# Attention, experts and dense layers in one kernel: position products by their reader, W1 pieces by the sum's copy, stacked products for the last head, tiles moved by 32 bytes

## The chip, the cores and the metric

The kernel runs on one core of a Trainium2 chip. The core has TensorE (products and transposes, in the profile PE, its weight loads PEld), VectorE (DVE), ScalarE (ACT), GpSimd (POOL) and SyncE (SP), which here issues DMAs; DMAs are also issued from ScalarE's and GpSimd's queues. The metric is the time of one execution on the device in microseconds; of several executions the median counts.

## The reference

Three stages follow one another: attention in which a query sees only keys of its own cluster, a top-1 mixture of experts with a capacity, and a gated dense layer. All data are float32.

```python
# attention: batch 2, heads 8, sequence 768, head size 64, 16 clusters
mask = q_assign[:, :, :, None] == k_assign[:, :, None, :]       # nearest centroid of each
scores = np.where(mask, scale * np.matmul(q, k.transpose(0, 1, 3, 2)), -1e9)
attn = np.exp(scores - scores.max(-1, keepdims=True))
attn = attn / (attn.sum(-1, keepdims=True) + 1e-09)
x = np.matmul(attn, v)             # -> 1536 tokens of 512
# experts: 8 experts, hidden size 1024, capacity 384
logits = x @ w_gate
expert_idx = np.argmax(logits, axis=1)
gate_w = softmax(logits)[np.arange(N), expert_idx]
# token i takes the next free place of its expert; beyond the capacity it is dropped
h = np.maximum(np.einsum('ecd,edf->ecf', disp, w1), 0.0)
y = np.einsum('ecf,efd->ecd', h, w2)
out[i] = gate_w[i] * y[expert_idx[i], pos[i]]
# dense: hidden size 1536
g, val = x @ w_gate2, x @ w_val
return (g * sigmoid(g) * val) @ w_out
```

## The kernel before

**Attention.** Sixteen heads go in eight pairs. The work runs in 96 blocks g of 128 queries of one head (six blocks for a head, in two halves of three). The order within a block is written out as a list of tokens (`S`, `E`, `Q`, `T0`, `T1`, `B0`, `O`, `V0`, `B1`), which `run` (L448) walks: `Q` issues the score products of a later block (`qk`, L332: TensorE, then the row maximum `nm` on VectorE, L352), `S` its exps (`soft`, L355, ScalarE, L362), `T0` and `T1` transpose the exps P of this block, three 128x128 pieces each, into one of two PSUM buffers called `t` (`pt`, L365; L378); ScalarE copies the first out (L381), VectorE the second (L383). `V0` multiplies three blocks' transposes with the values (`pv`, L385): keys 0 to 383 add up on partitions 0 to 63 of `acc`, keys 384 to 767 on partitions 64 to 127. `E` adds the two (`evac`, L400): ScalarE copies the lower half to `ol` (L408), VectorE adds the upper (L410) into O, which holds two heads. `O` multiplies O with R, an identity beside the router's weights (`onat`, L414): out come the tokens' rows and their share of the router's logits.

**Routing.** Tokens are routed in four parts u = 0 to 3 of 384, each when the eight heads of its half sequence are done. `route` (L639) is a generator: `run` takes one step of it in each block (trickle, L503), so a chain is spread over some 16 blocks. It sums the logits over heads, finds the maximum, the one-hot rows `oh`, the gate `gw`, and the places: small products count the tokens of the same expert ahead of each token (L669 to L672). They are written into a `t` buffer when `oh` is done; VectorE reads that at L677, four steps on. Then x is scaled by the gate on ScalarE (L686) and GpSimd scatters the rows to memory (L624), and `offsets` (L697) turns the counts into places in memory. The parts 0 and 1 are routed in the middle of attention, 2 near its end, and 3 behind it: at the end of `run` the last two heads' second half is summed and multiplied (six copies with a scale on ScalarE instead of one product on VectorE, L435), with transposes of the identity as warming products in the gaps (`warm`, L442).

**Experts.** Weights come from memory in raw pieces of 512 KB in four buffers (`load`, L836), and are split in a high and a low part: ScalarE casts to W1h or W2h, VectorE or GpSimd subtracts (`split`, L846; half pieces for the first expert's W1 by `piece`, L857, one in each of the blocks 85 to 92). A product of two such numbers is three products, added in PSUM. `rows` (L868) loads an expert's tokens (`xr`), `xt` (L884) transposes them, twelve 128x128 pieces, into two banks and splits them into X; an `If` on the expert's count chooses the width 208 or 384 here, and 176, 208 or 384 in the layers (`arms`, L906). The 384-wide arm issues three products (`prod`, L916), the narrow arms two with the high and the low operand side by side (`both`, L925: 416 and 208 columns, or 352 and 176). `run` (L988) orders the experts: W1 in four steps (`l1`), W2 (`l2`). On SyncE's queue stand the raw loads, the first expert's rows (L876, two DMAs), two more raw loads, and the loads of counts into registers (L1007).

**Dense layers.** `gv` (L1130) multiplies the experts' outputs Yh and Yl with two weights (L1145), `o` (L1156) the hidden ghh and ghl with the last (L1165), all 512 columns wide.

**Places.** In the built program right-side tiles before the change start at multiples of 64 bytes within a partition: exps P 155584, their transposes PT 177088, the score operands Ak 118720 and Aq 106432, X 174784, H 187072, ghh 162496. The left side holds the weights, W1h 37984, W1l 54368, W2h 70752, W2l 87136, and Yh 103520, Yl 132192, each 32 past a multiple of 64.

Of the kernel before, what the change touches and what calls it, by code (L numbers as in the profile page):

```python
# [23 lines left out]
class Attention:  # L24


    def __init__(self, tc, ctx, q, k, v, cent, gate, keep, ident, raw):
# [30 lines left out]
        self.R = self.v1.tile([128, H // 2, 2 * D + 2 * E], F32, name="R")  # L58
        self.cbd = one.tile([128, H // 2, 2 * C], F32, name="cbd")
# [49 lines left out]
    def unit(self, gate):  # L109

        nc, ident = self.nc, self.ident
        H, D, E = self.H, self.D, self.E
        nc.gpsimd.memset(self.R[:, :, 2 * D:], 0.0)
        for r in range(2):
            o, c = slice(r * D, (r + 1) * D), slice(2 * D + r * E, 2 * D + (r + 1) * E)
            nc.sync.dma_start(out=self.R[o, :, c], in_=gate.rearrange("(h r d) e -> d r h e", d=D, r=2)[:, r])
        nc.gpsimd.tensor_copy(self.R[:, :, 0:2 * D], ident.unsqueeze(1).to_broadcast([128, H // 2, 2 * D]))

# [281 lines left out]
    def evac(self, G):  # L400
# [5 lines left out]
        acc = self.heads[hd]["acc"]  # L406
        ol = self.v1.tile([D, HS], F32, tag="ol", name="ol")
# [6 lines left out]
    def onat(self, n, half, act=None):  # L414
# [14 lines left out]
        x = self.x[2 * b + half][:, :, 2 * hp * D:2 * (hp + 1) * D].rearrange("p j (r d) -> p j r d", r=2)  # L429
        for dst, c, w in ((self.lg[:, b, js, 2 * hp:2 * hp + 2, :], 2 * D, E),  # L430
                          (x, 0, D)):
            if act and w == D:
                for jj in range(HJ):
                    for r in range(2):
                        act.activation(out=x[:, jj, r], in_=ps[:, jj, r * D:(r + 1) * D], func=AF.Copy,  # L435
                                       scale=rs[:, jj, r:r + 1])
                yield True
                return
            yield nc.vector.tensor_tensor(out=dst, in0=ps[:, :, c:c + 2 * w].rearrange("p j (r d) -> p j r d", r=2),
                                          in1=rs.unsqueeze(3).to_broadcast([128, HJ, 2, w]), op=ALU.mult)  # L440

# [6 lines left out]
    def run(self, cent, gate, early, fill, after, spare):  # L448
# [90 lines left out]
        assert not bg  # L539
        G, n = 2 * NH - 1, self.NP - 1  # L540
        (_, r), = chains
        assert not moves
        while next(r) is not True:
            pass
        self.pv(G)
        on = self.onat(n, 1, nc.scalar)
        for q, k in ((on, 2), (r, 9)):
            for _ in range(k):
                next(q)
        self.warm(self.ps_s, "s", 10)  # L550
# [3 lines left out]
        next(on)  # L554
        last = after(n, 1, lambda: self.warm(self.ps_s, "s", 16))
        next(last)
        for q in (on, last):
            for _ in q:
                pass
# [5 lines left out]
class Router:  # L565
# [73 lines left out]
    def route(self, u, sb, ps, idle=None):  # L639
# [16 lines left out]
        yield v.tensor_reduce(out=lo, in_=self.lg[:, b, js].rearrange("p j h e -> p j e h"), axis=AX.X, op=ALU.add)  # L656
        yield v.tensor_reduce(out=mx, in_=lo, axis=AX.X, op=ALU.max)
        yield v.tensor_tensor(out=d, in0=lo, in1=bc(mx), op=ALU.subtract)
        for j in range(J):
# [4 lines left out]
        yield v.tensor_tensor(out=oh, in0=t, in1=bc(m2), op=ALU.is_equal)  # L664
        if idle:
            idle()
        pt = ps.tile([128, J, 128], F32, tag="t", name="t")
        pp = pt.rearrange("p j t -> p (j t)")[:, 0:J * E].rearrange("p (j e) -> p j e", j=J)
        nc.tensor.matmul(flat(pp), lhsT=self.before, rhs=flat(oh), start=True, stop=False)  # L669
        for k in range(1, J):  # L670
            nc.tensor.matmul(flat(pp[:, k:]), lhsT=self.all, rhs=flat(oh[:, 0:J - k]), start=False, stop=False)
# [4 lines left out]
        yield True  # L676
# [108 lines left out]
class Experts:  # L785
# [50 lines left out]
    def load(self, i):  # L836
# [6 lines left out]
        self.nc.sync.dma_start(out=t, in_=src)  # L843
        self.loads[e, i] = t

    def split(self, e, i, low=None):  # L846
# [6 lines left out]
        j = (low or (nc.vector if i < 4 else nc.gpsimd)).tensor_tensor(out=l, in0=t, in1=h.bitcast(F32), op=ALU.subtract)  # L853
        self.load(8 * e + i + NRAW)
# [13 lines left out]
    def rows(self, e):  # L868
# [6 lines left out]
        for q, a, b in ((nc.sync, 0, 1), (nc.sync, 1, 3)) if e == 0 else ((nc.scalar, 0, 3),):  # L875
# [8 lines left out]
    def xt(self, e, cnt):  # L884
        nc = self.nc
        banks = []
        for kp in range(self.KD // 2):
            ps = self.bank("xp")
            for kk in range(2):
                c = (kp * 2 + kk) * 128  # L890
                for t in range(self.nt):
                    nc.tensor.transpose(ps[:, kk, t * 128:(t + 1) * 128], self.xr[e][:, t, c:c + 128], self.ident)
            banks.append(ps)

        def body(w):
            for kp, ps in enumerate(banks):
                h, l = [self.X[:, i, 2 * kp:2 * kp + 2, 0:w] for i in range(2)]
                nc.scalar.copy(out=h, in_=ps[:, :, 0:w])  # L898
                nc.vector.tensor_tensor(out=l, in0=ps[:, :, 0:w], in1=h.bitcast(F32), op=ALU.subtract)
# [66 lines left out]
    def l1(self, mp, cnt, last):  # L966
# [3 lines left out]
        def body(w):  # L970
            if last is not None:
# [310 lines left out]
```

## Time and profile before

| | before |
|---|---|
| median of three runs | 781.29 us (779.28 to 782.27) |
| profiled execution | 779.61 us |
| its span in the trace | 777.9 us |
| TensorE products | 751.8 us, 97% |
| weight loads | 624.7 us, 80% |
| VectorE | 513.7 us, 66% |
| ScalarE | 400.9 us, 52% |
| GpSimd | 272.1 us, 35% |
| granted clock over the span | 0.993 |

The span lies between the first and the last instruction; what is left of an execution, 1.7 us here, lies around it. Attention takes roughly the first 272 us, the experts the time up to about 500, the dense layers the rest. A busy share is an average over these stages: which wait matters is read from the waits and from the chain that ended last.

### The profile page before, as it was taken

The numbers are of one execution on the slowest core, as the hardware profiler recorded it, in microseconds if no ns is written. First come the engines' busy times: TensorE is split into PE (matmuls) and PEld (weight loads), VectorE is DVE, ScalarE is ACT, GpSimd is POOL, SyncE is SP. The second block draws the span as 40 slices with busy tenths as digits, with TensorE's granted clock in tenths as the row PEclk, the third lists the DMA queues.
The fourth block names the chain that finished last, engine by engine and source line by source line (L and its number), as shares of the span: only waits on it lengthen the run. The fifth ranks groups of instructions, "written<-read, shape, count | busy, mean of one in ns | idle before, by whom it ended". The sixth has DMA issues, their size and how long they took to land.

```text
span 777.9 us, 12611 instructions
## 1 busy us (share of the span) xinstructions
PE 751.8 (97%) x4298; PEld 624.7 (80%) x4298; DVE 513.7 (66%) x856; ACT 400.9 (52%) x772; POOL 272.1 (35%) x251
## 2 busy tenths in 40 slices
PE   8999999998999989999999999999999999999996
PEld 8777777776776679989999998788888888888885
DVE  4667778786786745667676655776667766767433
ACT  5777776776776844667666633444222232222110
POOL 6120220211221565444493432444223333233244
PEclk9999999999999999999999999999999999999999
DMA  8837768527153443777777632232122121110012
GB/s 202 211 81 202 197 191 236 133 72 183 41 153 119 149 151 108 254 241 248 259 248 250 215 110 82 82 108 82 55 65 71 56 80 55 55 54 1 1 54 109
DMA packets 93339, 102.35 MB, mean 132 GB/s; under 512 B 30304, under 2 KB 77408, under 8 KB 93248
## 3 DMA queue, kind: packets, MB, share of 16 engines
q1 hardware_dynamic: 88384, 89.33, 39.8%
q0 software_dynamic: 1920, 6.29, 2.2%
q10 hardware_dynamic: 2944, 5.54, 2.1%
q8 instruction: 55, 0.90, 0.5%
q14 instruction: 36, 0.29, 0.1%
HBM read 68.21 MB, written 12.58 MB: 104 GB/s over the span
## 4 chain that ended last, share of the span: by engine, by line
PE 77%; DVE 7%; ACT 7%; DMA 3%; issue 3%; POOL 1%; ACTq 0%; DVEq 0%; SPq 0%; POOLq 0%
PE o L1165 12%; PE g L1145 11%; PE v L1145 11%; PE acc L397 8%; PE s L349 8%; PE t L378 7%; PE yp L930 3%; PE hp L930 3%; PE hp L922 2%; PE yp L922 2%; ACT P L362 2%; DMA raw<-in_moe_w 2%; PE yp L931 2%; PE hp L931 2%; DMA xr<-moe_rows 1%
## 5 line engine op out<-in xcount | busy, mean ns | idle before, releaser
L352 DVE TENSOR_REDUCE nm<-s 128x1 f32<-128x768 f32 x96 | 91.1, 950 | 13.0 <-PE s L349 11.0
L853 POOL TENSOR_TENSOR W2l<-raw,W2h 128x1024 fp32r<-128x1024 f32 x30 | 71.5, 2401 | 79.9 <-ACT W2h L852 79.8
L362 ACT ACTIVATE P<-s,nm 128x768 f32<-128x768 f32 x96 | 86.5, 902 | 12.0 <-DVE nm L352 10.3
L378 PE MATMUL t<-ident,P 128*128 128x128 f32 x576 | 83.6, 276 | 5.8 <-ACT PT L381 5.1
L378 PEld LDWEIGHTS t<-ident,P 128*128 128x128 f32 x576 | 68.5, 141 | 15.4 <-ACT PT L381 7.2
L1154 POOL TENSOR_TENSOR ghl<-u,ghh 128x512 fp32r<-128x512 f32 x36 | 50.0, 1389 | 76.1 <-ACT ghh L1153 76.1
L397 PE MATMUL acc<-PT,ldv 128*64 128x384 f32 x384 | 69.0, 494 | 0.0
L930 PE MATMUL yp<-H,W2h 128*128 128x416 f32 (+1 forms) x224 | 65.4, 363 | 1.1 <-DVE hp L944 0.8
L930 PE MATMUL hp<-X,W1h 128*128 128x416 f32 (+1 forms) x224 | 65.3, 362 | 0.7 <-ACT X L898 0.7
L1173 DVE TENSOR_TENSOR acc<-o,acc 128x512 f32<-128x512 f32 x60 | 41.5, 691 | 33.4 <-PE o L1165 33.2
L349 PE MATMUL s<-Ak,Aq 128*128 128x384 f32 x192 | 58.8, 387 | 4.1 <-ACT P L362 4.0
L381 ACT COPY PT<-t 128x384 f32<-128x384 f32 x96 | 45.8, 477 | 31.1 <-PE t L378 29.8
L1151 DVE TENSOR_TENSOR u<-sg,g 128x512 f32<-128x512 f32 x36 | 24.8, 688 | 54.4 <-ACT sg L1150 51.6
L1153 ACT CAST ghh<-u 128x512 fp32r<-128x512 f32 x36 | 22.4, 622 | 68.2 <-DVE u L1152 68.2
L931 PE MATMUL hp<-X,W1l 128*128 128x208 f32 (+1 forms) x224 | 56.6, 253 | 0.1
L931 PE MATMUL yp<-H,W2l 128*128 128x208 f32 (+1 forms) x224 | 56.4, 252 | 0.0
L383 DVE COPY PT<-t 128x384 f32<-128x384 f32 x96 | 52.5, 547 | 4.5 <-PE t L378 4.5
L853 DVE TENSOR_TENSOR W1l<-raw,W1h 128x1024 fp32r<-128x1024 f32 x28 | 44.3, 1602 | 13.2 <-ACT W1h L852 12.8
L349 PEld LDWEIGHTS s<-Ak,Aq 128*128 128x128 f32 x192 | 29.1, 190 | 28.5 <-ACT P L362 17.5
L349 PE MATMUL s<-kB,qB 80*128 80x384 f32 (+1 forms) x192 | 50.6, 344 | 0.8 <-ACT kB L284 0.7
L410 DVE TENSOR_TENSOR O<-acc,ol 64x384 f32<-64x384 f32 x32 | 17.6, 550 | 45.7 <-ACT ol L408 45.7
L397 PEld LDWEIGHTS acc<-PT,ldv 128*64 128x64 f32 x384 | 24.8, 136 | 28.1 <-issue 28.0
(256 smaller groups left out, 1918.9 us busy)
## 6 DMA issues: line engine op xcount, KB each, us to landing
raw<-in_moe_w SPq DMA_DIRECT2D x64, 512.0 KB, 4.6
Ak<-Hk SPq DMA_DIRECT2D x32, 192.0 KB, 4.1
moe_rows<-zero SPq DMA_DIRECT2D x8, 768.0 KB, 4.8
raw<-in_moe_w_gate SPq DMA_DIRECT2D x12, 512.0 KB, 3.4
raw<-in_moe_w_val SPq DMA_DIRECT2D x12, 512.0 KB, 3.4
raw<-in_moe_w_out SPq DMA_DIRECT2D x12, 512.0 KB, 3.3
xr<-moe_rows ACTq DMA_DIRECT2D x7, 768.0 KB, 6.6
ldq<-in_q SPq DMA_DIRECT2D x16, 192.0 KB, 3.8
```

Source lines behind the costliest of these rows:

```text
L349: nc.tensor.matmul(ps[:, c, 0:HS], lhsT=ql[:, qs], rhs=kr[:, c * HS:(c + 1) * HS], start=a == 0, stop=a == 1)
L352: nc.vector.tensor_reduce(out=nm, in_=ps[:, :, 0:HS], axis=AX.XY, op=ALU.max, negate=True)
L362: nc.scalar.activation(out=P, in_=ps[:, :, 0:HS], func=AF.Exp, bias=nm, accum_out=self.pairs[n]["sum"][:, i, r:r + 1])
L378: nc.tensor.transpose(ps[:, jj, :], P[:, a, jj * 128:(jj + 1) * 128], self.ident)
L383: nc.vector.tensor_copy(PT[:, js, cs], ps)
L397: nc.tensor.matmul(acc[c * D:(c + 1) * D], lhsT=v[:, c * HJ + j], rhs=PT[:, c * HJ + j, :], start=j == 0, stop=j == HJ - 1, tile_position= ...
L853: j = (low or (nc.vector if i < 4 else nc.gpsimd)).tensor_tensor(out=l, in0=t, in1=h.bitcast(F32), op=ALU.subtract)
L930: self.nc.tensor.matmul(out[:, :, 0:w], lhsT=W[0][:, k, cols], rhs=mov[:, :, k, 0:w], start=k == 0, stop=False)
L931: self.nc.tensor.matmul(out[:, 0, 0:w], lhsT=W[1][:, k, cols], rhs=mov[:, 0, k, 0:w], start=False, stop=k == ks - 1)
L1145: nc.tensor.matmul(p, lhsT=W[a], rhs=self.Y[b][:, k, ts], start=i == 0, stop=i == 3 * self.KD - 1)
L1154: nc.gpsimd.tensor_tensor(out=hl[:, fc], in0=u, in1=hh[:, fc].bitcast(F32), op=ALU.subtract)
L1165: nc.tensor.matmul(p[t], lhsT=h[a][:, fc, t * 128:(t + 1) * 128], rhs=W[b][:, fc], start=fc == 0 and i == 0, stop=fc == 1 and i == 2)
```

## The change

Five edits. (1) In `route` the position products move from behind `oh` to right in front of their reader; the product with the running sum comes first and is left out for u = 0. (2) The eight W1 half pieces move to the token `E` of the blocks 85, 88, 91 and 94: one before the sum's copy and one behind it. (3) The second half of the last two heads: `evac` copies all of `acc` with one ScalarE instruction, and `ends` multiplies it with R2, in which the identity and the gate's rows stand twice, one below the other, so that the product over 128 partitions adds the two halves of the keys; the first of the two heads' logits is summed ahead (`lo7`), so that the chain's first step is an add of 24 elements. (4) The first expert's rows come in three DMAs; only two thirds are transposed ahead, the last third in the 384-wide arm; X is split in the arms of the first `l1`; the two raw loads behind the rows wait for the last transpose, and the second expert's rows are loaded behind the first `l1`. (5) A tile of 32 bytes is put first on the right side.

```diff
+        self.R2 = self.v1.tile([128, 2, D + E], F32, name="R2")
...
     def evac(self, G):
...
+        if n + 1 == self.NP and half == 1:
+            self.sums.append(self.v1.tile([128, HS], F32, name=f"oa{r}"))
+            nc.scalar.copy(out=self.sums[r], in_=acc)
+            return
...
+    def ends(self, r):
+        ps = self.ps_m.tile([128, HJ, D + E], F32, tag="mm", name="on")
+        for jj in range(HJ):
+            self.nc.tensor.matmul(ps[:, jj, :], lhsT=self.sums[r][:, jj * 128:(jj + 1) * 128], rhs=self.R2[:, r],
+                                  start=True, stop=True)
+        return ps
+    def logits(self, ps, r):
+        self.nc.vector.tensor_tensor(out=self.lg[:, self.B - 1, HJ:J, H - 2 + r], in0=ps[:, :, D:D + E],
+                                     in1=self.rs2[:, :, r:r + 1].to_broadcast([128, HJ, E]), op=ALU.mult)
+    def copies(self, ps, r):
+        for jj in range(self.J // 2):
+            self.nc.scalar.activation(out=self.x[-1][:, jj, (H - 2 + r) * D:(H - 1 + r) * D], in_=ps[:, jj, 0:D], func=AF.Copy,
+                                      scale=self.rs2[:, jj, r:r + 1])
...
                 elif tok == "E" and c == CFG["ec"] and G >= 0:
+                    for st in pieces[:1] if g >= self.free else ():
+                        pieces.pop(0)()
                     self.evac(G)
+                    for st in pieces[:1] if g >= self.free else ():
+                        pieces.pop(0)()
...
+        ps = self.ends(0)
         while next(r) is not True:
             pass
         self.pv(G)
-        on = self.onat(n, 1, nc.scalar)
...
+        self.logits(ps, 0)
+        v.tensor_reduce(out=lo7, in_=self.lg[:, self.B - 1, HJ:J, 0:self.H - 1].rearrange("p j h e -> p j e h"), axis=AX.X,
+                        op=ALU.add)
+        self.copies(ps, 0)
+        for _ in range(10):
+            next(r)
+        self.warm(self.ps_s, "s", 4)
         self.evac(G)
         for _ in r:
             pass
+        ps = self.ends(1)
+        self.logits(ps, 1)
+        for _ in after(n, 1, lambda: self.warm(self.ps_s, "s", 8), lo7, lambda: self.copies(ps, 1)):
+            pass
...
+    def route(self, u, sb, ps, idle=None, lo7=None, copies=None):
...
         yield v.tensor_tensor(out=oh, in0=t, in1=bc(m2), op=ALU.is_equal)
+        yield v.tensor_tensor(out=t, in0=oh.bitcast(F32), in1=self.edump[:, us], op=ALU.mult)
+        yield v.tensor_reduce(out=et, in_=t, axis=AX.X, op=ALU.add)
+        yield v.reciprocal(out=gw, in_=se)
...
-        nc.tensor.matmul(flat(pp), lhsT=self.before, rhs=flat(oh), start=True, stop=False)
+        if u:
+            nc.tensor.matmul(flat(pp), lhsT=self.all, rhs=flat(self.sum), start=True, stop=False)
+        nc.tensor.matmul(flat(pp), lhsT=self.before, rhs=flat(oh), start=u == 0, stop=False)
         for k in range(1, J):
...
-        nc.tensor.matmul(flat(pp), lhsT=self.all, rhs=flat(self.sum), start=False, stop=True)
-        yield v.tensor_tensor(out=t, in0=oh.bitcast(F32), in1=self.edump[:, us], op=ALU.mult)
-        yield v.tensor_reduce(out=et, in_=t, axis=AX.X, op=ALU.add)
-        yield v.reciprocal(out=gw, in_=se)
-        yield True
+        if u == 2:
+            yield True
         yield v.tensor_tensor(out=t, in0=pp, in1=oh.bitcast(F32), op=ALU.mult)
...
     def xt(self, e, cnt):
+        if e == 0:
+            def first(w):
+                for k in range(self.KD if w == WIDE else 0):
+                    turn(2, k)
+                body(w, ((0, 1), (1, 2), (2, 4)))
+            i = [turn(t, k) for t in range(2) for k in range(self.KD)][-1]
+            return first, i
...
-        self.xt(0, cnt)
+        start, last = self.xt(0, cnt)
+        for i in range(4, 6):
+            rt.after(self.load(i + NRAW), [last])
...
+            pad = c2.enter_context(tc.tile_pool(name="pad", bufs=1, side="right"))
+            pad.tile([128, 8], F32, name="pad")
             keep = {n: c2.enter_context(tc.tile_pool(name=f"keep{n}", bufs=n, side="right")) for n in (1, 2, 3)}
```

In the built program after the change P, PT, Ak, Aq, X, H and ghh all start 32 bytes past a multiple of 64 (P 151776, PT 173280, X 174624, H 186912, ghh 162336); the weights and Y stand where they stood.

Where instructions move, three places show it. The first is TensorE around the first chain's position products. `t<-roh` and `t<-sum` are those products, `s` the scores, `t<-ident,P` the transposes of P, `on` the products with R; before:

```order
L212 MATMUL asp<-Xk,cbd 32x384
L669 MATMUL t<-roh,before 128x24
L671 MATMUL t<-roh,all 128x16
L671 MATMUL t<-roh,all 128x8
L672 MATMUL t<-sum,all 128x24
L349 MATMUL s<-Ak,Aq 128x384 x2
L349 MATMUL s<-kB_110,qB_108 128x384 x2
L378 MATMUL t<-ident,P 128x128 x6
L427 MATMUL on<-R,O 128x144 x3
```

and after:

```order
L228 MATMUL ast<-ident,as 128x128 x3
L403 MATMUL acc<-PT,ldv 64x384 x6
L355 MATMUL s<-Ak,Aq 128x384 x2
L355 MATMUL s<-kB_114,qB_112 128x384 x2
L384 MATMUL t<-ident,P 128x128 x6
L713 MATMUL t<-roh,before 128x24
L715 MATMUL t<-roh,all 128x16
L715 MATMUL t<-roh,all 128x8
L355 MATMUL s<-Ak,Aq 128x384 x2
```

They come three groups of transposes later and are three instead of four.

The second is ScalarE at the end of attention: `P` are the exps, `PT` the copies of transposes, `ol` and `oa` the copies of sums, `rlo` and `rse` the router's exps and their sums, `x_97` (after: `x_101`) the rows being scaled, `tmp` the last part's rows; before:

```order
L362 ACTIVATE P,sum<-s,nm 128x768
L408 COPY ol<-acc 64x384
L381 COPY PT<-t 128x3x128
L660 ACTIVATE rlo,rse<-rd 128x8 x3
L661 ACTIVATE rse<-rse,eps 128x3
L381 COPY PT<-t 128x3x128
L686 ACTIVATE x_97<-x_97,rgw 128x512
L408 COPY ol<-acc 64x384
L686 ACTIVATE x_97<-x_97,rgw 128x512 x2
L435 ACTIVATE tmp<-on,rs 128x64 x6
```

and after:

```order
L904 CAST W1h<-raw 128x2x256
L415 COPY oa_3389<-acc 128x384
L904 CAST W1h<-raw 128x2x256
L387 COPY PT<-t 128x3x128
L699 ACTIVATE rlo,rse<-rd 128x8 x3
L700 ACTIVATE rse<-rse,eps 128x3
L387 COPY PT<-t 128x3x128
L463 ACTIVATE tmp<-on,rs_3441 128x64 x3
L727 ACTIVATE x_101<-x_101,rgw 128x512 x2
L415 COPY oa_3468<-acc 128x384
L727 ACTIVATE x_101<-x_101,rgw 128x512
L463 ACTIVATE tmp<-on,rs_3441 128x64 x3
```

Two casts now stand around the copy of the sum; three of six copies into `tmp` stand ahead of the scalings, and two scalings ahead of the last sum's copy.

The third is SyncE's queue around the first expert's rows; before:

```order
L843 DMA raw<-in_moe_w 128x4x256 x8
L876 DMA xr<-moe_rows 128x512
L876 DMA xr<-moe_rows 128x2x512
L843 DMA raw<-in_moe_w 128x4x256 x2
L1007 TENSOR_LOAD offi
```

and after:

```order
L885 DMA raw<-in_moe_w 128x4x256 x8
L918 DMA xr<-moe_rows 128x512 x3
L1063 TENSOR_LOAD offi
L885 DMA raw<-in_moe_w 128x4x256 x2
L1063 TENSOR_LOAD offi
```

The load of a count into a register now stands ahead of the two raw loads.

## Rows read from the trace of the kernel before

**Rows 1.** Stretches with each engine's busy time, granted clock, DMA share.
```profile
core 0: us, PE busy (x) PEld busy (x) DVE busy (x) ACT busy (x) POOL busy (x), PEclk, DMA share, GB/s
272.00:293.00 21.00, 18.02 (x119) 14.53 (x119) 10.46 (x47) 9.48 (x24) 14.81 (x18) 1.00 0.47 162
498.00:763.00 265.00, 264.38 (x1152) 216.55 (x1153) 169.70 (x236) 78.25 (x136) 89.07 (x72) 1.00 0.17 56
```

**Rows 2.** TensorE's waits, whole span: total us, times, longest.
```profile
PE t L378 <- ACT PT L381: 5.1, 9, 0.6
```

**Rows 3.** Timeline, first chain: start, us, engine, instruction [wait <- releaser].
```profile
180.81 0.28 PE L669 MATMUL t<-roh,before 128*128 128x24 f32 x1
...
183.12 0.55 PE L378 MATMUL t<-ident,P 128*128 128x128 f32 x3 [0.57 <-ACT PT L381]
...
195.21 0.17 DVE L677 TENSOR_TENSOR rt<-t,roh 128x24 f32<-128x24 f32 x1
```

**Rows 4.** Timeline, second chain's last such wait.
```profile
242.19 0.55 PE L378 MATMUL t<-ident,P 128*128 128x128 f32 x3 [0.57 <-ACT PT L381]
```

**Rows 5.** Chain that ended last, in attention: start, us, what.
```profile
122.40 2.09 PE acc L397 x12
...
153.14 2.09 PE acc L397 x12
...
219.65 2.09 PE acc L397 x12
```

**Rows 6.** Groups of instructions, ScalarE, 245 to 272: busy us, mean ns.
```profile
L862 ACT CAST W1h<-raw 128x512 fp32r<-128x512 f32 x8 | 5.0, 629 | 0.0
L686 ACT ACTIVATE x<-x,rgw 128x512 f32<-128x512 f32 x3 | 2.2, 727 | 0.0
```

**Rows 7.** Timeline of the last blocks of attention.
```profile
269.87 0.48 ACT L381 COPY PT<-t 128x384 f32<-128x384 f32 x1
...
270.40 1.19 PE L378 MATMUL t<-ident,P 128*128 128x128 f32 x6 [0.52 <-ACT PT L381]
...
274.93 0.55 DVE L410 TENSOR_TENSOR O<-acc,ol 64x384 f32<-64x384 f32 x1 [0.91 <-ACT ol L408]
```

**Rows 8.** Chain that ended last, turn-over to the experts.
```profile
275.63 0.93 PE on L427 x6
276.82 1.33 ACT tmp L435 x6
278.15 0.57 ACT rlo L660 x6
...
286.87 3.83 DMA xr<-moe_rows
290.74 1.44 PE xp L892 x11
...
292.82 0.43 PE hp L930
```

**Rows 9.** Timeline of the turn-over and the first expert.
```profile
289.13 0.30 PE L892 MATMUL xp<-ident,xr 128*128 128x128 f32 x1 [0.74 <-DMA xr<-moe_rows]
...
306.28 1.08 ACT L852 CAST W1h<-raw 128x1024 fp32r<-128x1024 f32 x1
```

**Rows 10.** Chain that ended last, experts and dense layers.
```profile
294.00 0.20 PE hp L930
294.21 0.10 PE hp L931
...
437.57 16.98 PE hp L922 x96
...
507.39 5.61 PE o L1165 x24
...
515.75 2.72 PE v L1145 x12
```

**Rows 11.** Groups of instructions, TensorE, 293 to 765.
```profile
L930 PE MATMUL yp<-H,W2h 128*128 128x416 f32 x128 | 38.9, 369 | 0.3
```

More of the change, by code (lines that the diff above doesn't have):

```diff
@@ L412, in evac, with onat @@
             del self.heads[hd]
[L414 removed]
+    def onat(self, n, half):
         nc = self.nc
@@ L446, in warm, with run @@
             self.nc.tensor.transpose(w[:, 0, :], self.ident, self.ident)
-    def run(self, cent, gate, early, fill, after, spare):
+    def run(self, cent, gate, early, fill, after, spare, pieces):
         nc = self.nc
@@ L538, in run @@
                 trickle(g, tok)
-        assert not bg
+        assert not bg and not pieces
         G, n = 2 * NH - 1, self.NP - 1
@@ L542, in run @@
         assert not moves
+        v, sums = nc.vector, self.pairs[n]["sum"]
+        ps = self.ends(0)
         while next(r) is not True:
@@ L545, in run @@
         self.pv(G)
-        on = self.onat(n, 1, nc.scalar)
[L547 to L550, printed above, removed]
+        self.rs2 = self.keep[1].tile([128, HJ, 2], F32, name="rs2")
+        lo7 = self.keep[1].tile([128, HJ, self.E], F32, name="lo7")
+        v.tensor_scalar(out=self.rs2, in0=sums[:, HJ:J], scalar1=1e-9, scalar2=None, op0=ALU.add)
+        v.reciprocal(out=self.rs2, in_=self.rs2)
+        self.logits(ps, 0)
[5 more added lines that the diff above has]
+        self.warm(self.ps_s, "s", 4)
         self.evac(G)
@@ L885, in xt, with turn, body @@
         nc = self.nc
[L886 to L899, printed above, removed]
+        banks = [self.bank("xp") for _ in range(self.KD // 2)]
+        def turn(t, k):
+            return nc.tensor.transpose(banks[k // 2][:, k % 2, t * 128:(t + 1) * 128],
+                                       self.xr[e][:, t, k * 128:(k + 1) * 128], self.ident)
+        def body(w, parts=((0, 2), (2, 4))):
+            for a, b in parts:
+                h, l = [self.X[:, i, a:b, 0:w] for i in range(2)]
+                ps = banks[a // 2][:, a % 2:a % 2 + b - a, 0:w]
+                nc.scalar.copy(out=h, in_=ps)
+                nc.vector.tensor_tensor(out=l, in0=ps, in1=h.bitcast(F32), op=ALU.subtract)
+        if e == 0:
+            assert MERGED[-1] <= 256
+            def first(w):
[4 more added lines that the diff above has]
+            return first, i
+        for k in range(self.KD):
+            for t in range(self.nt):
+                turn(t, k)
         with self.tc.If(cnt > MERGED[-1]) as c:
@@ L1022, in run @@
             for mp in range(4):
-                ps = self.l1(mp, cnt, ps)
+                ps = self.l1(mp, cnt, ps, start)
+                start = None
+                if e == 0 and mp == 0:
+                    self.rows(1)
                 if mp < 2 and e:
@@ L1228, in tile_clustered_attention_moe_swiglu, with after @@
                 ex = Experts(tc, rt, w1, w2, ident, raw, keep)
-                def after(n, half, idle=None):
+                def after(n, half, *late):
                     b, hp = divmod(n, H // 2)
-                    return rt.route(2 * b + half, keep[2], at.ps_t, idle) if hp == H // 2 - 1 else None
+                    return rt.route(2 * b + half, keep[2], at.ps_t, *late) if hp == H // 2 - 1 else None
                 def first():
@@ L1240, in tile_clustered_attention_moe_swiglu @@
                 g0 = 2 * J * (at.NP - 2) + 9
-                spare = {g0: [first]}
-                for i in range(NRAW):
-                    for h in range(2):
-                        spare[g0 + 4 + 2 * i + h] = [lambda i=i, h=h: ex.piece(i, h)]
-                at.run(cent, gate, rt.setup, rt.fill, after, spare)
+                at.free = g0 + 4
+                pieces = [lambda i=i, h=h: ex.piece(i, h) for i in range(NRAW) for h in range(2)]
+                at.run(cent, gate, rt.setup, rt.fill, after, {g0: [first]}, pieces)
             at.stages[1].close()
```

54 lines of the change are left out of this document (28 added, 26 removed).

## The prediction

> **What bounds the kernel now.** I read the page's busy shares first, then the stretches, then the waits of TensorE, then the chain that ended last. TensorE bounds nearly everything: in the 265 us of experts and dense layers it is busy 264.38 us, while in the 21 us between attention and experts it has 18.02 us of work (warming products among them) and every other engine less [rows 1]. So there are two kinds of place where the time can move: waits of TensorE inside attention and in the 21 us of turn-over, and the pace of its products. An engine off TensorE's path is worth nothing by itself.
>
> The waits of TensorE over the whole span have one large regular entry: transposes that wait for ScalarE's copy of the block before, nine times, 5.1 us [rows 2]. The clock is granted in full in both stretches of [rows 1], so no term below is one of the clock.
>
> **Part one, the position products, -5.5 us.** Each routing chain writes its four small position products into one of the two PSUM buffers that the transposes of P use, and its reader on VectorE comes four of the chain's steps later, at one step a block. For the first chain the buffer is written at 180.81 and read at 195.21; in between T1 has no second buffer and waits 0.57 us for ScalarE's copy of T0 [rows 3]. There are four such waits in this hold (183.13, 186.00, 190.75, 193.07) and four in the second chain's, the last at 242.19 [rows 4]. The ninth wait of [rows 2] is another matter (270.40, at the end). Between the chains, and before the first, there is none.
> The waits alone give 8 x 0.57 = 4.6 us. A second view: one pair of heads takes 153.14 - 122.40 = 30.74 us without a chain's hold, and the two pairs that hold the first chain 219.65 - 153.14 = 66.51, which is 5.03 over twice 30.74 [rows 5]. In that stand the four products (under 0.7 us, which remain) and whatever else a chain costs; so a hold costs 2.3 to 4.4 us and both 4.6 to 8.8. I take 5.5, nearer to the waits, since they are counted one by one. Moved behind the chain's other steps the products stand in front of their reader: the buffer is held for a fraction of a block. New is a wait on VectorE: the reader now waits for TensorE's products, and behind it stands the row maximum of the next block, for which an exp waits. The four products take under 0.7 us, at most one T1 in a chain still waits, so the lower end is 4.6 - 2 x 0.57 = 3.4.
>
> **Part two, W1 pieces and the last half's sum, -0.2 us.** The eight casts of 0.63 us on ScalarE [rows 6] keep their number and go from one a block to two beside each of four copies of a sum. In the three earlier places ScalarE has a block's time to catch up; I cost them at nothing, and their price if the cover is gone is one cast each, 1.9. In the last place two casts, 1.25 us, stand around the sum's copy ahead of the copy of transposes that ran at 269.87 and for which TensorE waited already [rows 7]. The three products of the new `ends` fill part of that: +0.75 (0 to 1.25).
> In the last half's chain, the add on VectorE behind the copy of the sum goes, -0.55 [rows 7]. Six products at 275.63 become three and narrower, -0.1 (bound 0.47, half of 0.93; I stay near nothing, since the wait for the copy of the sum sets their start and the logits need them all). Then six copies (1.33 us) stood before the exps at 278.15, 1.59 us after the end of the products at 276.56 [rows 8]; with three copies ahead, and a difference that is four VectorE steps of about 0.2 us behind the products, the exps can start after 0.85: -0.74. Against it the copy of the second sum stands behind two scalings of x (0.73 us each [rows 6]) where it stood behind one, +0.4 (0 to 0.73). Sum 0.75 - 0.55 - 0.1 - 0.74 + 0.4 = -0.24, taken as -0.2, bounds -1.2 to +1.0. The warming products dropped (10 to 4, 16 to 8) lie in TensorE's idle time.
>
> **Part three, the first expert's rows, -1.7 us.** The rows come as 256 KB and 512 KB; the second transfer takes 3.83 us and lands at 290.70, eleven transposes (1.44 us) follow, and the first product starts at 292.82 [rows 8]. The first transfer, asked for in the same moment, was there for the transpose at 289.13 [rows 9], so 256 KB take some 2.2 us and 512 KB 3.83. Cut in three, the second third should land in between, near 289.9, 0.8 earlier; the third is only needed in the widest arm. Four transposes fewer, at 1.44 / 11 = 0.13 each, give 0.5, and the first cast covers one step of four instead of two, about 0.4. Sum -1.7; the lower bound, -1.0, is that the parts land together and only the work shrinks, the upper -2.1 that the second lands right behind the first. The two raw loads that stood behind the rows on SyncE now wait for the last transpose, some 2.7 us later; the next expert's first cast, which reads the first of them, runs at 306.28 [rows 9], so with a transfer of some 4 us (this kernel's 512 KB took 3.83) about ten us of cover remain. The next rows' DMA on ScalarE's queue moves behind the first products; nothing reads it for tens of microseconds.
>
> **Part four, the 32 bytes, -3.9 us.** They move every tile on the right side, in attention and afterwards, and no tile on the left. The weights stood and stand 32 bytes past a multiple of 64. Before, X, H and the hidden tiles of the dense layer stood at a multiple; after, they too stand 32 past. What that is worth no row shows by itself, but three rows stand on the two sides. The products of the first dense layer, where both operands stand 32 past already, take 2.72 / 12 = 226.7 ns for 512 columns. Those of the second, with one operand at each place, take 5.61 / 24 = 233.8, and they are 512 columns too [rows 10]. The 384-wide products of the experts, one operand at each place, take 16.98 / 96 = 176.9, against 2.09 / 12 = 174.2 in attention, where both operands stand at a multiple [rows 5, 10]. If it is the mixture that costs, 432 products of the second layer gain 7.1 ns, -3.1, and 192 of the wide ones 2.7 to 4, -0.8 by the upper: -3.9. In the narrow arms I take nothing: a pair of 416 and 208 columns takes 0.30 us [rows 10], where the pace of 512 and 384 columns (52.5 ns for 128, so 0.41 a column) would give 187 + 102 = 289 ns, but these 0.30 repeat without the scatter of the others and look set by something else than the place. Nothing in attention should change, since there both operands move together.
> The rows set a difference of 3% beside a difference of 32 bytes, no more. [...]
>
> **Sum.** -5.5 - 0.2 - 1.7 - 3.9 = -11.3. The profiled execution took 779.61 us (span 777.9), the median of the runs is 781.29, 0.2% above it; I carry the difference: 781.29 - 11.3 = **770.0 us**.
>
> **Rivals.** First, the pad does nothing: the excess of the second layer comes from its readers or its GpSimd-written operand. Then 770.0 + 3.9 = 773.9. For it speaks that no row has the same product at two places; against it, that 24 of 24 products in a row are slow and 12 of 12 of the other layer are not.
> Second, the pad speeds up the narrow pairs too. At 10.5 ns a pair, of which there are 256 with 416 columns (two rows like that of [rows 11]) and 192 with 352: -4.7, so 765.3; with twice that for the shorter pairs 763. Against it speaks that the 0.30 does not scatter.
> Third, the hold isn't given back: T1's waits go, but the exps and maxima behind the reader come late by as much, as ScalarE or VectorE sets the block's pace. 770.0 + 5.5 = 775.5. For it speaks that ScalarE and VectorE are two thirds full in attention; against it that pairs without a hold run at 30.74.
> Fourth, slower: the place 32 past is itself the slow one for an operand that TensorE streams, and what is slow in the second layer is its moving weights. Then the scores (384 products), the weighted sums (384), the narrow pairs (896 products) and the 192 wide ones pay 7.1 ns: 1856 x 7.1 = 13.2, and the 3.9 isn't won: 770.0 + 3.9 + 13.2 = 787.1. It turns the result to slower from (785.2 - 773.9) / 1856 = 6.1 ns a product on. Against it: the first dense layer streams from 32 past at the best pace there is.
>
> **How the numbers follow.** Chances: the forecast 0.36, the pad idle 0.32, the narrow pairs faster 0.10, the hold not given back 0.10, hold and pad both without effect (779.4) 0.06, the fourth 0.06. The forecast's own range, with part one from -3.4 to -8.8, part two from +1.0 to -1.2, part three from -1.0 to -2.1, is some 5 us to either side when the parts don't all err together by their bounds: 766 to 773.5. The range to hold 8 in 10 reaches to the first, second and third rivals: 763 to 777. What a measurement of this kernel can tell from no change is about 0.5%, 3.9 us: under 777.4 is faster, over 785.2 slower. Faster are the first four cases without the upper edge of the third rival (0.04): 0.84; no change 0.10; slower 0.06.
>
> **What would show it.** Right: no waits of T1 for ScalarE in the middle of attention, and the two pairs of [rows 5] near 63 us; the first product of the experts some 4.3 us behind the request of its rows instead of 292.82 - 286.87 = 5.95; 24 products of the second dense layer in 5.44 us. Wrong: the same number of waits under the reader's or another name; TensorE's last weighted sum later by more than a microsecond behind ScalarE's casts; the second layer still at 5.61 (first rival), the narrow pair under 0.30 (second), 384-wide products in attention above 174 ns (fourth).

## The result, and the profile after

The changed kernel takes 771.19 us (median of four runs, 769.47 to 772.23) where the kernel before takes 780.28 beside it (778.23 to 782.27): a ratio of 0.988, 95% interval 0.985 to 0.992, 9.1 us faster. The forecast was 770.0, the range 763 to 777; it was counted down from 781.29, the median of the first three of these four runs of before, and from 780.28 the same sum gives 769.0. The profiled execution of after took 771.29 us, its span 769.4; against 779.61 and 777.9 that is 8.3 and 8.5 us. The terms of the sum fared less well than the sum, as a table by stage shows. It gives the length of each stage in both traces, from TensorE's products that begin it:

| stage of the span | before | after | change | forecast |
|---|---|---|---|---|
| start to the first weighted sum | 29.84 | 29.73 | -0.11 | 0 |
| to the last weighted sum ahead of the first hold | 123.23 | 123.38 | +0.15 | 0 |
| to the fourth-last weighted sum (both holds) | 98.59 | 92.85 | -5.74 | -5.5 |
| to the product that counts the tokens (pieces, stacked sum) | 28.95 | 27.64 | -1.31 | -0.2 |
| to the first product of the experts (rows) | 12.21 | 10.70 | -1.51 | -1.7 |
| to the first expert's second layer | 11.26 | 14.08 | +2.82 | 0 |
| to the dense layers | 167.26 | 167.24 | -0.02 | -0.8 |
| to the end | 306.56 | 303.83 | -2.73 | -3.1 |

TensorE's waits over the whole span, in us in total, times, longest; the row of [rows 2] is gone:

```profile
PE s L355 <- ACT P L368: 4.1, 9, 1.4
...
PE hp L984 <- DVE X L939: 0.9, 2, 0.7
```

The timeline answers to [rows 3 to 5]. The first chain's products run 0.6 us ahead of their reader where it was 14.4, and from one sum at 153.11 to the one at 245.96 it is 92.85 us; the two pairs of [rows 5], 66.51 us before, take 63.45. The reader of the second chain's products, at 233.74, waits 1.86 us for them on VectorE:

```profile
153.11 0.54 PE L403 MATMUL acc<-PT,ldv 128*64 128x384 f32 x2
...
188.94 0.28 PE L713 MATMUL t<-roh,before 128*128 128x24 f32 x1 [0.24 <-ACT PT L387]
...
189.55 0.17 DVE L718 TENSOR_TENSOR rt<-t,roh 128x24 f32<-128x24 f32 x1
...
233.74 0.18 DVE L718 TENSOR_TENSOR rt<-t,roh 128x24 f32<-128x24 f32 x1 [1.86 <-PE t L715]
...
245.96 0.54 PE L403 MATMUL acc<-PT,ldv 128*64 128x384 f32 x2
```

The turn-over, against [rows 7 to 9]. The exps start 0.90 us behind the end of the stacked products (270.06 to 270.96); before, the timeline has 1.47 us there (276.54 to 278.01, 1.59 by the chain of [rows 8]):

```profile
275.54 1.00 PE L427 MATMUL on<-R,O 128*128 128x144 f32 x6
...
278.01 0.24 ACT L660 ACTIVATE rlo<-rd 128x8 f32<-128x8 f32 x1
```

After the change the rows are transposed from 282.39, and the first product of the experts follows after 1.91 us instead of 3.69. Then TensorE waits again at 290.14, in the second step of the first layer, for the end of the first step's work on VectorE; no such wait stands in the second step in the trace of before. The lines of after:

```profile
268.64 0.48 ACT L415 COPY oa<-acc 128x384 f32<-128x384 f32 x1
...
269.17 0.89 PE L449 MATMUL on<-R,oa 128*128 128x72 f32 x6
...
270.96 0.21 ACT L699 ACTIVATE rlo<-rd 128x8 f32<-128x8 f32 x1
...
273.60 0.24 PE L742 MATMUL xp<-sum,all 128*128 128x8 f32 x1
...
284.30 0.43 PE L984 MATMUL hp<-X,W1h 128*128 128x416 f32 x1 [0.70 <-DVE X L939]
...
290.14 0.43 PE L984 MATMUL hp<-X,W1h 128*128 128x416 f32 x1 [0.72 <-DVE hp L998]
...
298.38 0.43 PE L984 MATMUL yp<-H,W2h 128*128 128x416 f32 x1
```

Two stretches of the same place, with the columns of [rows 1]: in the second, of 3.2 us, the granted clock is 0.50, with TensorE busy for 3.04 us; in the 2.8 us ahead the clock is 0.98 and TensorE was busy for 1.71:

```profile
282.00:284.80 2.80, 1.71 (x10) 1.13 (x10) 0.62 (x2) 0.94 (x3) 2.80 (x3) 0.98 0.39 141
284.80:288.00 3.20, 3.04 (x12) 2.83 (x11) 0.72 (x2) 0.13 (x1) 3.20 (x3) 0.50 0.99 320
```

The chain that ended last, as [rows 10]: the 384-wide products took 16.98 and take 16.66, the second dense layer 5.61 and 5.49, the first 2.72 both times:

```profile
432.49 16.66 PE hp L976 x96
...
501.22 5.49 PE o L1227 x24
506.72 2.72 PE g L1207 x12
```

### The profile page after: what moved, and what is told of

Its sections match the earlier page's. It is cut to its first block, busy times and chain, and to the rows that moved or that the text cites. A ratio compares the mean times of both kernels' runs of the same rounds, so it can differ in the third digit from the quotient of the medians.

```text
span 769.4 us, 12587 instructions
## 1 busy us (share of the span) xinstructions
PE 745.8 (97%) x4285; PEld 622.9 (81%) x4285; DVE 513.5 (67%) x857; ACT 400.9 (52%) x773; POOL 272.7 (35%) x253
## 4 chain that ended last, share of the span: by engine, by line
PE 47%; DVE 5%; ACT 3%; issue 2%; DMA 2%; POOL 1%; ACTq 0%; DVEq 0%; POOLq 0%
PE o L1227 12%; PE g L1207 11%; PE v L1207 11%; PE yp L984 3%; PE hp L976 2%; PE yp L976 2%; PE hp L984 2%; DMA raw<-in_moe_w 2%; PE yp L985 2%; ACT W1h L893 1%; DVE gtmp L1185 1%; PE hp L985 1%; POOL out L1238 1%; DVE W1l L894 1%; PE xp L931 1%
## 5 line engine op out<-in xcount | busy, mean ns | idle before, releaser
L384 PE MATMUL t<-ident,P 128*128 128x128 f32 x576 | 81.8, 277 | 1.3 <-DVE rm L702 0.7
L984 PE MATMUL hp<-X,W1h 128*128 128x416 f32 (+1 forms) x224 | 67.3, 371 | 1.6 <-DVE X L939 0.9
L1185 DVE SCALAR_TENSOR_TENSOR gtmp<-raw,gtmp 128x512 uint32<-128x512 uint32 x36 | 45.4, 1261 | 1.2
```

The source lines that it names most:

```text
L384: nc.tensor.transpose(ps[:, jj, :], P[:, a, jj * 128:(jj + 1) * 128], self.ident)
L984: self.nc.tensor.matmul(out[:, :, 0:w], lhsT=W[0][:, k, cols], rhs=mov[:, :, k, 0:w], start=k == 0, stop=False)
L1185: v.scalar_tensor_tensor(out=b, in0=Hw, scalar=0xC0000000, in1=b, op0=ALU.bitwise_and, op1=ALU.bitwise_or)
```

## The experiments

Each run stands beside runs of the kernel before on its chip, whose medians were 781.58 (runs 1 to 4), 781.26 (5 to 8) and 780.21 (9 to 12). Executions of one kernel differ by several us (777.70 to 784.02 in fourteen runs of the kernel before), 2.6 of which can come from one stretch at the start (last section), so stages of the traces are compared rather than totals. Totals of different kernels that lie 1 us apart tell nothing.

**The position products alone (run 3).** The kernel before with the new order in `route` and nothing else.

```diff
-        nc.tensor.matmul(flat(pp), lhsT=self.before, rhs=flat(oh), start=True, stop=False)
...
         yield v.reciprocal(out=gw, in_=se)
...
+        if u:
+            nc.tensor.matmul(flat(pp), lhsT=self.all, rhs=flat(self.sum), start=True, stop=False)
+        nc.tensor.matmul(flat(pp), lhsT=self.before, rhs=flat(oh), start=u == 0, stop=False)
...
         yield v.tensor_tensor(out=t, in0=pp, in1=oh.bitcast(F32), op=ALU.mult)
```

> The kernel before with the position products alone moved in front of their reader (the sum's product first, none for the first part). Theory (the held buffer was the whole loss): eight waits of T1 for ScalarE's copy gone, last weighted sum 5.6 us earlier, 774.7. Rival 1 (only the waits come back): -4.6, 775.7. Rival 2 (the gain in the change's attention came from the W1 pieces' new places): under 2 us, 778.5.

It took 773.84 us, ratio 0.991 (0.988 to 0.994). The stage with both holds takes 245.38 - 152.85 = 92.53 us against 98.59, -6.06, and of the eight waits for the copy of T0 none is left; TensorE's waits between 150 and 250 us:

```profile
PE s L349 <- ACT P L362: 1.5, 4, 0.7
PE t L674 <- ACT PT L381: 0.2, 1, 0.2
PE t L378 <- DVE PT L383: 0.2, 1, 0.2
```

So this edit alone brings what the stage brings in the change, and 1.5 us more than the waits add up to. The timeline shows where the rest stood: in a block with such a wait it takes longer from the start of the transposes to the start of the next products than the idle time says. The same block, in the kernel before and in this run:

```profile
182.06 0.49 PE L378 MATMUL t<-ident,P 128*128 128x128 f32 x3
...
183.50 0.90 PE L427 MATMUL on<-R,O 128*128 128x144 f32 x6
```

```profile
181.43 0.82 PE L378 MATMUL t<-ident,P 128*128 128x128 f32 x6
182.09 0.90 PE L427 MATMUL on<-R,O 128*128 128x144 f32 x6
```

With the wait it is 1.44 us, without it 0.66. The eight blocks with a wait take 1.36 to 1.59 us, 11.5 in all, where eight without take 5.3: 6.2 us, of which 4.6 show as idle time of TensorE.

**The W1 pieces (run 7).** The changed kernel with the half pieces back at one a block.

```diff
-                pieces = [lambda i=i, h=h: ex.piece(i, h) for i in range(NRAW) for h in range(2)]
+                        spare[g0 + 4 + 2 * i + h] = [lambda i=i, h=h: ex.piece(i, h)]
```

> The changed kernel with the W1 half pieces back at one a block, in the blocks 85 to 92. Theory (two casts around the sum's copy of block 94 cost what ScalarE has there in spare, nothing, and free the other blocks of nothing that was short): last weighted sum within 0.2 us of 266.4, 771.2. Rival (the term of the sum, +0.75 in the last blocks against -0.3 in the others): 0.5 us faster.

771.32 us, 0.988 (0.984 to 0.991). From the sum at 245.81 to the counting product at 273.45 it is 27.64 us, as in the changed kernel to the hundredth. The two places are worth the same for the stage, but not within it. With one piece a block the last weighted sum starts 20.22 us behind the first of these four and not 20.44, 0.23 earlier, a little more than the theory allowed; behind it the stage is 0.23 longer (7.43 against 7.20). In both kernels the copy of the second sum starts 1.83 us behind the three copies ahead of it on ScalarE (266.67 to 268.50, and 266.81 to 268.64), so the earlier sum waits for ScalarE's scalings. With the position products alone the stage takes 28.81 us, so all of its 1.2 us belongs to the stacked sum and the edits that go with it.

**The first expert's rows (run 4).** The changed kernel with the rows, transposes and split of X as before.

```diff
-        for q, a, b in ((nc.sync, 0, 1), (nc.sync, 1, 2), (nc.sync, 2, 3)) if e == 0 ...
+        for q, a, b in ((nc.sync, 0, 1), (nc.sync, 1, 3)) if e == 0 ...
...
-        start, last = self.xt(0, cnt)
-        for i in range(4, 6):
-            rt.after(self.load(i + NRAW), [last])
+        self.xt(0, cnt)
...
```

> The changed kernel with the rows, transposes and split of the first expert as before (two DMAs, twelve transposes, X split in a region of its own, raw loads behind the rows). Theory (the early start is given back inside the first expert by a half clock, by the finer waits for X and by a new wait of 0.72 us for the end of the region in which X is written): first product 1.5 us later, but the first expert's first layer 9.7 us long and not 12.5, so 1.3 us faster, 769.9. Rival (that loss is there whatever the rows do, since the idle time ahead of the transposes sets the clock): 1.5 us slower, 772.7.

771.06 us, 0.988 (0.985 to 0.991), within noise of the changed kernel. Neither case came as told, since here too the clock fell to half in the first expert's products (0.56 over the stretch from 284.50 to 288.00, 0.50 from 285.14 to 287.14), so that the first layer did not get back to its old length:

```profile
284.50:288.00 3.50, 3.50 (x15) 3.40 (x15) 0.13 (x1) 0.00 (x0) 2.78 (x2) 0.56 0.70 229
```

It fell also in the kernel before with the position products alone (0.50 from 285.19 to 287.19), and not in the kernel before (1.00 from 275 to 300). So the half clock is not the new rows' doing, as the rival had it, and it hides what else they cost. The next two runs part the two.

**Warming products (run 5), and a region for X (run 6).** The changed kernel with more warming products; and, apart from that, with X split in a region of branches ahead of the first layer's.

```diff
-        for i in range(26):
+        for i in range(30):
...
         start, last = self.xt(0, cnt)
+        for i in range(5):
+            nc.tensor.transpose(w[:, 0:128], self.ident, self.ident)
```

> The changed kernel with four more 512-wide warming products ahead of the first expert's transposes and five warming transposes behind them. Theory (TensorE's idle time around the transposes is what lets the granted clock fall to half for some 3.2 us of the first expert's first products): the clock stays at 1.00 there, first product to the second expert's transposes 12.55 down to about 11, 1.6 us faster, 769.6. Rival (the clock falls for another reason, or the warming products push the transposes back by as much): no gain, 771.2.

```diff
+        self.arms(cnt, start)
+        start = None
         for e in range(E):
```

> The changed kernel with X split in a region of branches of its own, ahead of the first layer's arms. Theory (the 0.72 us wait in the second step of the first layer is a wait for the end of the region in which X is written): that wait is gone, one branch more ahead of the first product, 0.3 to 0.7 faster. Rival (it is a wait for a PSUM bank): it stays.

The first took 770.9 us, 0.988 (0.984 to 0.991), the second 768.79 in its one run. Stretches of the first, to lay beside those of the changed kernel:

```profile
282.00:284.80 2.80, 2.63 (x17) 1.68 (x15) 0.66 (x2) 0.98 (x3) 2.80 (x3) 1.00 0.42 149
284.80:288.00 3.20, 2.98 (x18) 2.69 (x18) 0.69 (x2) 0.41 (x2) 3.20 (x3) 1.00 0.96 324
```

The clock stays up, and from the counting product to the first expert's second layer it is 23.52 us instead of 24.78; the medians of 770.9 and 771.19 don't show these 1.3 us. In the second run the wait for the end of the region is gone; of TensorE's waits for these instructions one is left, ahead of the first product:

```profile
284.80 0.43 PE L984 MATMUL hp<-X,W1h 128*128 128x416 f32 x1 [1.34 <-DVE X L939]
```

It waits longer there (1.34 against 0.70) and is done earlier: 22.70 us, with the clock at 1.00 though TensorE idles more than in the changed kernel (it is busy for 1.77 of the 4 us from 280.70, and there for 2.27 of the 4 us from 280.60). So the wait at 290.14 is one for the region in which X is written, as expected; and idle time around the transposes is not what alone brings the clock down. That run 5 kept the clock by its warming products is therefore not shown. Over all kernels this stretch reads:

| rows of the first expert | clock 1.00 | clock at half for some 3 us |
|---|---|---|
| as before | 23.47 (before), 23.51 (run 2) | 24.72 (run 3), 25.86 (run 4), 24.78 (run 11) |
| as changed | 23.52 (5), 23.58 (8), 23.35 (12) | 24.78 (after), 24.76 (1), 24.98 (7) |
| as changed, X in a region of its own | 22.70 (6), 22.69 (9), 22.99 (10) | |

At the same clock the new rows gain nothing as they stand: what they win ahead of the first product they give back behind it. In run 8, with the clock at 1.00, it is 12.89 us from the first product to the second layer where it was 11.26 before: 0.9 of the 1.6 at the second step's wait, the rest in the first step, whose products wait for the parts of X. With X in its own region they gain 0.8.

**The 32 bytes (runs 1, 2, 8, 11, 12).** The changed kernel without the tile, and the kernel before with it alone.

```diff
-            pad = c2.enter_context(tc.tile_pool(name="pad", bufs=1, side="right"))
-            pad.tile([128, 8], F32, name="pad")
```

> The changed kernel without the 32-byte tile: right-side tiles start at multiples of 64 again. Theory (a product's pace depends on where its two operands start): 24 products of the second dense layer go back from 5.49 to 5.61 us, 96 wide ones from 16.66 to 16.98, the first dense layer stays at 2.72 for 12, narrow pairs go back to 300 ns; in all about +2.5 us, 773.7. Rival (the tile does nothing, the layer is faster because something else moved): 5.49 and 16.66 stay, 771.2.

> The kernel before with the 32-byte tile alone. Theory: 5.49 us for 24 and 16.66 for 96, about -2.5 us, 777.8; attention up to the last weighted sum as before (start of the last sum at 272.2). Rival (the tile does nothing alone): 780.3.

Without the tile 772.51 us, 0.989 (0.986 to 0.992); with it alone 780.35, 0.999 (0.998 to 1.001). Of what was expected of the second the 96 wide products came (16.66), the second layer did not. The chain of the first and that of the second, 24 products of the second dense layer:

```profile
501.35 5.59 PE o L1227 x24
```

```profile
506.97 5.60 PE o L1165 x24
```

Alone the tile brings nothing in the second layer, although both operands then stand 32 past a multiple of 64; in the changed kernel it brings 5.59 to 5.49. The two kernels also differ in two small tiles that are kept to the end (`rs2` and `lo7`) and move X, H and the hidden tiles by another 128 bytes: within 512 bytes the hidden tiles start at 192 (before), 160 (run 2), 64 (run 1) and 32 (changed), and the weights always at 96. The first dense layer has both operands at 96. Hence the next runs: 480 bytes in the changed kernel and 96 in the kernel before put X, H and the hidden tiles at 96, and 96 bytes in the changed kernel at 480, which is the same place within 128 bytes but not within 512.

```diff
-            pad.tile([128, 8], F32, name="pad")
+            pad.tile([128, 120], F32, name="pad")
```

> The changed kernel with 480 bytes instead of 32: X, H and the hidden tiles then start 96 past a multiple of 512, where the weights and Y start. Theory (products run at full pace where all operands have the same place within 512 bytes, as in the first dense layer): 24 products of the second layer in 5.44 instead of 5.49, 96 wide ones in 16.66, a narrow pair of 416 and 208 at or under 0.300, about 1.6 us faster, 769.6. Rival (no such rule; 32 is a place that happens to suit the second layer): 5.6 for 24, 2 us slower, 773.2.

> The kernel before with a tile of 96 bytes, which puts X, H and the hidden tiles 96 past a multiple of 512, where the weights stand (32 bytes, the second run, put them at 160). Theory (same place within 512 bytes): 24 products of the second layer 5.45 instead of 5.61 us, narrow pairs at or under 300 and 271, about 3 us faster from the first expert's second layer to the end, 777.5. Rival (the place within 512 bytes is not what decides): 5.6, 780.3.

> The changed kernel with 96 bytes instead of 32: right-side tiles then start 480 past a multiple of 512, the same place as the weights within 128 bytes but not within 512. If 128 bytes is what counts, 24 products of the second layer take 5.45 us; if 512 bytes, 5.5 to 5.6.

768.16 us, 0.984 (0.980 to 0.988); 777.42, 0.997 (0.9945 to 1.0001, so its total alone settles nothing); 770.96 in one run. The same 24 products, in this order:

```profile
514.81 5.44 PE o L1227 x24
```

```profile
508.42 5.44 PE o L1165 x24
```

```profile
515.71 5.59 PE o L1227 x24
```

At the weights' place within 512 bytes the second layer runs at the pace of the first, 226.7 ns, in both kernels; the same place within 128 does not do it (5.59 us for 24). Whether 256 would do, and whether the equality counts or the place 96 by itself, these runs don't part, since the weights stand at 96 in all of them. The dense layers, 306.56 us before and 303.83 changed, take 302.99 in run 8 and 303.37 in run 11.

**Together (runs 9 and 10).** 480 bytes with X in its own region, and with the warming products as well.

> The changed kernel with 480 bytes instead of 32 and X split in a region of its own. Theory (both gains stand side by side: products at 226.7 ns where operands stand at the same place within 512 bytes, no 0.72 us wait, clock full if the idle time falls well): second layer 5.45 for 24, from the offsets to the first expert's second layer some 22.7 us instead of 24.8, in all 767 to 768. Rival (the half clock comes back by chance of timing): 1.3 more, 769.

> The same with the warming products of the fifth run as well. Theory (they take the chance out of the clock): the clock at 1.00 through the first expert, 22.4 to 22.8 us from the offsets to the first expert's second layer, 767.0. Rival (they push the first product back by as much): 768.3.

768.07 us, 0.986 (0.983 to 0.989), and 768.31, 0.985 (0.983 to 0.987). TensorE's waits for X in the first's turn-over and first expert, one where the changed kernel had two and the one at 290.14:

```profile
PE hp L984 <- DVE X L939: 1.3, 1, 1.3
```

Both beat both kernels, the changed one by 3 us. The stages give 0.8 of it to the region and 0.8 to the place; 1.3 is the half clock, which the profile of the changed kernel has and these two don't. The warming products add nothing here, as the rival had it: the clock is at 1.00 in either trace, and the stretch of the table above is 0.3 us longer with them.

## Why the prediction was right, and where it was not

**Position products: right, by the mechanism named.** -5.5 forecast, -5.74 in the change, -6.06 alone. The count of waits was the lower and the spacing the upper view, and the truth lay between them: a wait's price was 0.78 us (1.44 against 0.66), where its idle time of 0.57 was counted. The wait of VectorE for the products that was priced as new is there, 1.86 us in the second chain (233.74); no wait of TensorE goes back to it. TensorE waits 0.24 us once ahead of the products.

**Pieces and stacked sum: -0.2 forecast, -1.3 measured.** The terms that failed are the two on the side of the losses: +0.75 for two casts ahead of the last copy of transposes, which put the last weighted sum 0.23 us later than in run 7 and the end of the stage no later, and the +0.4 for the second sum's copy behind two scalings, which came as 0.04 (it starts 2.24 us behind the start of the last weighted sum, and started 2.20). They were added, but the one delay lies under the other. From the last weighted sum to the products on it is 2.77 us where it was 3.32: the whole add of 0.55 won, nothing given back. The products came as -0.1 as forecast (1.00 to 0.89 us), the exps' term, -0.74, as -0.57.

**The first expert's rows: right up to the first product, wrong after it.** -1.51 against -1.7 there. What failed is the step that took the split of X as shorter work at the same waits. X is cast and subtracted in three parts one behind the other, the first products wait for the parts (0.9 us in two waits), and since X is now written inside the first step's arms, the second step waits for the last VectorE instruction of those arms, 0.72 us. At the same clock the stretch takes 23.5 us before and after. The half clock, 1.3 us more in this profile, comes and goes with either form of the rows; it was no part of the prediction.

**The 32 bytes: -3.9 forecast, -2.8 in the stages in which they act, and for another reason.** What failed is the step from three rows to "mixture within 64 bytes": run 2 has no mixture by that measure and no gain. The wide products' term, -0.8, came as -0.64 but is not the place's alone: 16.66 us stands also in the kernel without the tile and in run 2, and 16.97 in run 7, whose right-side tiles stand where the changed kernel's do. The chain of run 1 and that of run 7:

```profile
432.52 16.66 PE hp L976 x96
```

```profile
432.57 16.97 PE hp L976 x96
```

In the dense layers the tile shows in the second alone: 5.59 without, 5.49 with it, 18 x 0.10 = 1.8 us. The other 0.9 of the 2.7 is there without the tile (305.62 us of dense layers in run 1 against 306.56). Of it 0.4 is a shorter wait for the experts' last output, which is no matter of places; in the kernel before and in the changed one:

```profile
PE g L1145 <- DVE Yl L961: 0.8, 1, 0.8
```

```profile
PE g L1207 <- DVE Yl L1015: 0.4, 1, 0.4
```

The wait is 0.8 in runs 2 and 11 too, which only move tiles. Another 0.4 stands in the second layer's products (101.98 us from start to start before, 101.59 in run 1), whose tiles moved from 192 to 64. The size of the forecast's term, -3.1, was right for operands at one place: at 96 these 432 products take 98.91 us (run 11), 3.07 less. The narrow pairs, taken at nothing, lost as much as the wide products won: from start to start a pair of 416 and 208 columns takes on average 303.5 ns in the first layer of the experts and 304.1 in the second, against 300.4 and 302.0, so 0.7 us for 256 of them. So the first rival was right that 32 bytes alone do nothing (5.60 us in run 2), and wrong about the cause: with the same readers and the same GpSimd-written operand the 24 products took 5.61 us with the hidden tiles at 192 (before) and 5.44 at 96 (run 11), 3% of a product's time.

**The sum held by luck, because its errors offset each other:** -1.1 by the stacked sum and -0.2 by the buffer, against +3.0 by the rows and the half clock and +1.1 by the bytes: 11.3 forecast, 8.5 in the spans. The +3.0 hold 1.3 of a half clock that other profiles of the same stage don't have.

## What to carry to other kernels

A PSUM buffer that was written early for a reader that came late cost TensorE four waits of 0.57 us in each of its two holds here; write it right ahead of its reader, and price the wait by how much longer a block with it takes (0.78 us here), since its idle time alone was a quarter short. With the split of X moved into the first step's arms, the second step waited 0.72 us for the last VectorE instruction of those arms, and at the same clock the stretch up to the second layer took 23.58 us (run 8) where it was 23.47 before: an early start can be given back a few microseconds on, so measure to the end of the stage. Where products are the bound, try the operands at the same place within 512 bytes: with both at 96, 24 products took 5.44 us here instead of 5.61, and one padding tile did it.

## What the runs showed of the hardware that was not expected

The same 24 products took 5.44 us with their operands at the same place within 512 bytes (four kernels), 5.49 at 32 against 96 and 5.59 to 5.61 at 64, 160, 192 and 480 against 96. What moved is the operand of the weight loads (`ghh` and `ghl`, 128x128 each); the other, the dense layer's weights at 512 columns, stood at 96 throughout. Why is not settled: nothing in a trace shows what a product waits for inside. The pace of the wide products isn't decided by the place alone, since two kernels with the same places differ (16.66 and 16.97 in the changed kernel and run 7).

The granted clock fell to half (0.50) for some 3 us in the first expert in the profiles of six of fourteen kernels, with more and with less idle time of TensorE ahead of it: in the 4 us before it fell TensorE was busy for 2.27 us in the changed kernel and for 1.43 in run 4, and in run 6, where it stayed at 1.00, for 1.77 ahead of the first product. By the table the fall cost 1.2 to 1.5 us, in one 2.4. Which executions fall was not settled. At the start of attention, between 10 and 30 us, it is granted at 0.83 in the profile of the changed kernel and at 1.00 in that of run 4, which differs from it only from the first expert's rows on; the first weighted sum starts at 29.73 and at 27.16. These 2.6 us are part of the spread between executions.
